# Keys and part of x transposed by DMA, and a rebuilt last batch, in a softcap attention with a routed attention layer behind it

## The chip, the cores and the metric

The kernel runs on one core of a Trainium2 chip. The metric is the device time of one execution in microseconds; a lower time is better. Engines are named as in the profile: PE is TensorE (the matrix engine) and PEld its weight loads, DVE is VectorE, ACT is ScalarE, POOL is GpSimd and SP is SyncE, whose queue issues nearly all DMAs.

## The reference

Two layers follow each other: softcap attention over 8 batches, 12 heads, 448 positions and 64 channels, and then a layer with four experts, each a small causal attention of its own, of which two are chosen for each token.

```python
scores = scale * np.matmul(q, k.transpose(0, 1, 3, 2))
scores = cap * np.tanh(scores / cap)
attn = softmax(scores)                       # max subtracted, sum + 1e-9
x = (attn @ v) laid out as [batch, 448, 12 * 64 = 768]

logits = x @ w_gate                          # 4 experts
topk = the two largest; w = softmax of these two
for e in range(4):
    q, k, v = x @ wq[e], x @ wk[e], x @ wv[e]
    a = softmax(causal(scale * q @ k.T))
    ye = a @ v @ wo[e]
    out += (e is chosen as first or second) * its w * ye
```

`out` is float32 of [8, 448, 768]. The inputs are float32; the kernel computes in float16 with float32 sums.

## The kernel before, in words

**Pairs.** The attention works on pairs of heads, six pairs to a batch, 48 in all. Pair p is step p of ACT, and two more steps follow (48 and 49, `NPV` is 50). For every step ACT runs three tanh (`tanh`, L768: the parts X, Y1 and Y2 of the scores) and one exp over all of them (`expo`, L780). The pairs of the last batch (42 to 47) only take 320 of their queries in their own steps (`W1`); the last 128 queries of all six are worked on in steps 48 and 49 (`pv2`).

**Feeding a pair.** `load` brings q, k and v of two pairs at once into a ring of four tiles each (`kf`, `qf`, `vf`); the last 64 keys come in small DMAs of their own (`ktf`, `vtf`). `cast` makes float16 of them on POOL. `tr` transposes the keys (`k16`, and `ktz` for the last 64) and the queries on PE into one PSUM bank; DVE copies the bank into `qk` in one instruction (L683). Rows were loaded so that one partition holds several neighbouring positions, and queries therefore stand permuted, within groups of 64, in `q16` and in `qk`. `fill` runs the score matmuls of a pair (`heads`, L717, and `tails`, L727).

**Finishing a pair.** `pv` multiplies the exps with the values (L795, L802) and DVE divides by the sum into `xk`. `xt` transposes `xk` on PE against a permutation that restores the order of the positions (`perm`, `pswap`, L841), and DVE copies the result into `xT` (L850), which holds one batch of x with channels on the partitions.

**The experts of a batch.** When a batch's six pairs are done, `b_v` (L910), `b_qk` (L937), `b_gate` and `b_mask` (POOL) prepare its values, keys, masked queries (`qm`, L951) and weights. The masks `mB` are transposed by a DMA into `mT` (`turned`, L389). Each batch has two expert score passes s = 0 and 1 (`b_score`, L1057), and each needs one ACT exp (L1066). The table `exps` says in which step of ACT these exps stand: for all but batch 6 five and six steps after the next batch begins, for batch 6 in steps 48 and 49. POOL zeroes what is not causal (`causal`, L1076, L1083). `b_pv` (L1116, L1131) gives `oB`, `b_ot` adds the two passes on POOL and has them transposed by DMA into `oT`, and `b_wo` (L1164) multiplies with wo: four tiles of 128 rows in two halves each, of which the last only stores its upper 64 rows because it overlaps the third. The results go through the four tiles `ob` to HBM (L1178).

**The last batch** has code of its own (`last`, `last2`, `normed`): projections (L1247, L1276, and L1390, L1400 for the last 128 rows), scores (L1300) on top of a mask that a matmul of `negm` puts into the bank first (L1290), exps (L1310), products (L1330, L1444), a division, transposes (L1208), a copy into `oTL` and the wo product (L1223). Its outputs go into the same tiles `ob` as batch 6's. Plain copies out of PSUM (`evac`, L377) go to DVE or, after ACT's fixed work, to ACT.

**The order.** Nothing is emitted in program order. Every operation goes into a graph (`Graph.op`) with an estimated cost. ACT's tanh and exp have a fixed order; all other operations get due times from it, partly given by hand as an offset to an ACT step (`due=(ref, ...)`). `solve` then simulates all engines and picks, for each, the ready operation that is due first. `SEEDS` and `JIT` add a pseudo-random offset to the due times, one seed for every 4 us of the simulated time. So a change of one cost or one operation moves the order of everything else. A DMA's simulated time is its wire time behind the DMAs before it (`wire`), and `occ` is its time on SP.

Of the kernel before, what the change touches and what calls it, by code (L numbers as in the profile page):

```python
# [16 lines left out]
SWITCH = 0.1  # L17
# [4 lines left out]
JIT = 0.784  # L22
SEEDS = (0, 0, 677, 325, 935, 794, 478, 0, 0, 908, 702, 455, 94, 0, 415, 476, 0, 612, 697, 64, 320, 0, 337, 707, 93, 0, 0, 917, 365, 771, 130, 0, 644, 11, 733, 810, 0, 8, 0, 0, 56, 391, 495, 0, 0, 0, 0, 0, 0, 579, 0, 0, 472, 59, 74, 554, 0, 0, 795, 949, 933, 285, 781, 323, 0, 548, 585, 976, 176, 0, 938, 86, 0, 0, 687, 0, 992, 980)
TWIRE = 0.2
TOCC = 0.18
# [3 lines left out]
KEEPN = 1  # L29
NFILL = 30  # L30
# [19 lines left out]
class Graph:  # L50
# [79 lines left out]
    def solve(self, when, banks, lent):  # L130
# [44 lines left out]
        while len(order) < n:  # L175
            best = None
            for e, rs in ready.items():
# [8 lines left out]
                def rank(x):  # L186
                    u = x[1]
                    if u.name[:4] == "gexp":
                        return -INF, 0.0, 0
                    d = u.due + lag if u.first or left < TAIL else max(u.due + lag, t0 + 1.223)  # L190
                    d -= 0.505 * (u.grp is not None and not u.opens and left >= TAIL)
# [5 lines left out]
                near = t0 + (0.007 if left >= TAIL else SWITCH + 0.02)  # L197
                t, o = min((x for x in c if x[0] <= near), key=rank)
                if e in ("PE", "DVE") and not o.first:
                    for t2, u in c:  # L200
                        if u.first and u.due + lag < t + o.occ + 0.0 and t2 < t + max(SWITCH + 0.01, min(o.occ, 0.25)):
# [68 lines left out]
def kernel(  # L270
# [116 lines left out]
    def turned(n, dst, src, r, w, name, due=None):  # L387
# [3 lines left out]
           wire=TWIRE * n, occ=0.4 + TOCC * n)  # L391
# [12 lines left out]
    vtz = [sb(f"vtz{i}", [128, 2, Dh + 1]) for i in range(NV)]  # L404
    qk = [sb(f"qk{i}", [128, S + 512]) for i in range(NQK)]
    yp = [sb(f"yp{i}", [128, 7, S]) for i in range(NYP)]
# [4 lines left out]
    xT = [sb(f"xT{i}", [128, NDC, S]) for i in range(2)]  # L411
# [7 lines left out]
    pB = [sb(f"pB{i}", [128, 64 + 1024]) for i in range(4)]  # L419
# [14 lines left out]
    negm = sb("negm", [128, W1])  # L434
# [6 lines left out]
    oTL = [sb(f"oTL{i}", [128, 2, 128]) for i in range(2)]  # L441
# [23 lines left out]
    def load(p, n):  # L465
# [13 lines left out]
        def tail(eng, dst, src, g):  # L479
# [4 lines left out]
        sp(lambda: full(kf[s][:, d], k[b, h, 0:KM], KC), w=w("kf"), name=f"ldk{p}", wire=0.8 * n)  # L484
        sp(lambda: nc_eng.dma_start(qf[s][:, d], q[b, h].rearrange("h (p c) d -> p h (c d)", c=QC)),
           w=w("qf"), name=f"ldq{p}", wire=0.95 * n)
# [8 lines left out]
        sp(lambda: full(vf[s][:, d], v[b, h, 0:KM], KC), w=w("vf"), name=f"ldv{p}", wire=0.8 * n)  # L495
# [39 lines left out]
    def setup_b():  # L535

# [21 lines left out]
        def lastc():  # L558
            nc.gpsimd.memset(vL[:, :, Dh : Dh + 1], 1.0)
            nc.gpsimd.memset(negm, 0.0)  # L560
# [3 lines left out]
        gp(0.9, lastc, w=["vL", "negm", "neg2"], due=150.0)  # L564
# [6 lines left out]
        gp(0.4, below(negm[:, 0:128], 0), ["negm"], ["negm"], due=150.0)  # L571
        gp(0.4, below(negm[:, W1 - 128 : W1], -64), ["negm"], ["negm"], due=150.0)
# [42 lines left out]
    def cast(p):  # L615
# [5 lines left out]

        def qc(e):
# [12 lines left out]
        gp(0.2, lambda: nc.gpsimd.tensor_copy(ktz[z], ktf[s][:, o].rearrange("p g d -> p (g d)")),  # L635
           [("ktf", x, 0), ("ktf", x, 1), ("zk", s)], [("ktz", z)], name=f"kt16_{p}")
# [10 lines left out]
    def tr(p):  # L647
# [29 lines left out]
        g = Group(AUX)  # L677
        pe(0, lambda: tk(g, (0, 1, 2)), kr + [("s", XB[0])] * (p == 1), [("tps", p, "k"), ("qkw", t)], g, occ=0.165, name=f"trk{p}")
# [27 lines left out]

    def heads(p, what):
        dst = X if what == "X" else Y
        ci = {"X": 0, "Y1": 1, "Y2": 2}[what]
        t = qk[of(p, what)[0] % NQK]  # L710
        n = wid(p)
        for c in (ci,) if p < NP else range(KC):
            for g in range(2):
# [4 lines left out]
                    dst[:, g, o], t[r, S + 128 * (c + 1) : S + 128 * (c + 2)], t[r, qs],  # L718
# [3 lines left out]
    def tails(p):  # L722
        for i, m in enumerate(of(p)):
# [3 lines left out]
            nc.tensor.matmul(X[:, 2, o], t[:, S : S + 128], t[:, qs], start=True, stop=True)  # L727

    def fill(p, what):
        def rd(p, what=None):  # L730
            return [y for m in of(p, what) for y in (
                ("qk", m % NQK, "k"), ("qk", m % NQK, "q"), ("qkw", m % NQK))]
# [12 lines left out]
        if what == "X":  # L745
            if p == 0:
                tr_first_tails()
            pe(wid(p), lambda: tails(p), rd(p) + [
                ("qk", m % NQK, "t") for m in of(p)], [("s", bs[2])], name=f"sT_{p}",
# [6 lines left out]
    exps = {HP * (b + 1) + (XOFF if b < LB - 1 else (6, 7))[s]: (b, s) for b in range(LB) for s in range(2)}  # L756
# [27 lines left out]
    def pv(p):  # L784
        if p >= NP:
            return pv2(p)
        y = yp[p % NYP]
# [3 lines left out]
        def mm(g, i, n, what):  # L791
            ps = bank(g)[:, 0 : 4 * (Dh + 1)].rearrange("p (n g d) -> p n g d", n=2, g=2)
            w = (WIN if p < PB else WIN1)[2 * i + n]
            if "X" in what:
                nc.tensor.matmul(  # L795
                    ps[:, n, :, :], y[:, 2, w : w + 128], vtz[u], start=(n == 0), stop=False,
# [3 lines left out]
            for c in cs:  # L800
                for h in range(2):
                    nc.tensor.matmul(  # L802
                        ps[:, n, h, :], y[:, SLOT[c][h], w : w + 128], v16[u][:, h, c, :],
# [3 lines left out]
        vr = [("v16", u), ("v16d", u), ("vtz", u), ("vtzd", u)]  # L807
# [23 lines left out]
    def xt(p, due=None):  # L831
        if p >= NP:
            return
        b, j = divmod(p, HP)
        g = Group(AUX)

        def mm():
            ps = bank16(g)
            for n in range(4 if p < PB else 3):
                w = 128 * n if p < PB else WIN1[n]  # L840
                nc.tensor.transpose(  # L841
                    ps[:, w : w + 128],
                    xk[p % NXK][:, n, :, :].rearrange("p g d -> p (g d)"),
                    perm if n < 3 else pswap,
# [8 lines left out]
    def pv2(p):  # L853
# [33 lines left out]
        def mt():  # L887
            for i in range(3):
                nc.tensor.transpose(
                    bank16(gt)[:, 128 * i : 128 * (i + 1)],  # L890
                    xk2[h][:, i].rearrange("p g d -> p (g d)"), perm)

        pe(0, mt, [("xk2", h), ("perm", 0), ("perm", 1)], [("xtp", p)], gt, occ=0.165, name=f"xt{p}")
# [8 lines left out]
    def b_v(b, ref):  # L902
        x = b % 2
        for n in range(4):
            g = Group(AUX + XB, 1.8)
            w = WIN[n]
            for j0 in (0, 2, 4):
                def mm(g=g, w=w, j0=j0):
# [8 lines left out]
                   due=(ref, 7.024 + 1.4 * n))  # L917
# [656 lines left out]
```

## Time and profile before

| what | value |
|---|---|
| median of 3 runs | 313.27 us (311.67 to 315.44) |
| the profiled execution | 314.04 us |
| its span | 312.0 us |
| busy share PE / DVE / ACT / POOL | 90% / 70% / 94% / 58% |
| mean granted clock of PE | 0.983 |
| read from HBM / written | 36.19 MB / 11.01 MB |

The span is the time from the first to the last thing that the profiler recorded; the profiled execution's own time has some 2 us around it. Busy shares are means over stages: the attention of 48 pairs fills the span but for a few microseconds ahead and the last batch's own work behind. In a row of the trace the first number is the start or a window, and a bracket at the end gives the idle time before the instruction and who ended it.

### The profile page before, as it was taken

Reading aid. Unit: us, or ns where it says so; the run is one execution under the profiler, and the core shown is the slowest. Engines: PE = TensorE matmul, PEld = TensorE weight load, DVE = VectorE, ACT = ScalarE, POOL = GpSimd, SP = SyncE. Lnnn points to the kernel's source line nnn. Section 1 sums busy time; section 2 is a strip of 40 time slices with the busy share of each in tenths; the row PEclk is TensorE's granted clock in tenths of the full one; section 3 lists DMA queues with packets and bytes.
Section 4 is the critical chain, followed back from the end, with each engine's and each line's share of the span. In section 5 each row is a group of like instructions: output and inputs, shape, how many; then the busy total and the mean of one; then the engine's idle time right before and its main releaser. Section 6 shows DMA issues by size and latency. Waiting matters only on the chain.

```text
span 312.0 us, 8950 instructions
## 1 busy us (share of the span) xinstructions
PE 280.9 (90%) x3476; PEld 190.4 (61%) x3476; DVE 217.8 (70%) x645; ACT 291.8 (94%) x246; POOL 181.4 (58%) x498
## 2 busy tenths in 40 slices
PE   7677689979898899989998999999999989999993
PEld 3354356658564766657655776568664866667761
DVE  2345556666764886869766877788776877786883
ACT  4699999998999999999999999999999999999562
POOL 7694436996787452984785576947866414701200
PEclk9979979998999999999999999999999999999999
DMA  6899999869976995789873698855014200531136
GB/s 183 182 227 221 297 272 253 220 168 268 251 189 159 313 272 159 187 179 255 217 164 78 201 310 196 129 162 154 2 41 146 97 2 19 87 120 60 36 148 207
DMA packets 87482, 53.29 MB, mean 171 GB/s; under 512 B 48144, under 2 KB 83728, under 8 KB 87440
## 3 DMA queue, kind: packets, MB, share of 16 engines
q1 hardware_dynamic: 87136, 52.49, 65.5%
q8 instruction: 27, 0.44, 0.6%
q10 hardware_dynamic: 304, 0.23, 0.2%
q14 instruction: 15, 0.12, 0.2%
HBM read 36.19 MB, written 11.01 MB: 151 GB/s over the span
## 4 chain that ended last, share of the span: by engine, by line
ACT 66%; PE 20%; DMA 4%; POOL 3%; issue 3%; DVE 2%; SPq 1%; ACTq 0%; POOLq 0%
ACT yp L768 34%; ACT yp L780 28%; ACT pB L1066 4%; PE A L1164 2%; DMA kf<-in_k_dram 2%; PE Y L717 2%; PE A L937 2%; PE A L910 2%; PE A L802 2%; DMA out_dram<-ob 2%; PE X L1057 1%; PE A L1116 1%; PE A L663 1%; PE A L795 1%; PE X L727 1%
## 5 line engine op out<-in xcount | busy, mean ns | idle before, releaser
L780 ACT ACTIVATE yp<-yp 128x3136 f16<-128x3136 f16 (+4 forms) x51 | 139.0, 2726 | 0.0
L768 ACT ACTIVATE yp<-Y 128x896 f16<-128x896 f32 (+2 forms) x100 | 94.6, 946 | 2.6 <-PE Y L717 2.6
L768 ACT ACTIVATE yp<-X 128x1344 f16<-128x1344 f32 (+2 forms) x50 | 65.1, 1302 | 2.5 <-PE X L727 1.5
L802 PE MATMUL A<-v,yp 128*128 128x65 f16 x1116 | 56.4, 194 | 0.0
L802 PEld LDWEIGHTS <-yp 128*128 128x128 f16 x1116 | 49.0, 98 | 5.7 <-issue 2.9
L795 PE MATMUL A<-vtz,yp 128*128 128x130 f16 x186 | 41.3, 222 | 7.9 <-ACT yp L780 3.7
L826 DVE TENSOR_TENSOR xk<-A,rca 128x256 f16<-128x256 f32 (+1 forms) x96 | 39.7, 415 | 2.9
L717 PE MATMUL Y<-qk 64*128 64x448 f16 (+2 forms) x216 | 36.2, 341 | 5.7 <-ACT yp L768 5.1
L639 POOL CAST v<-vf 128x384 f16<-128x384 f32 x48 | 24.6, 514 | 27.0 <-PE A L802 22.1
L620 POOL CAST k<-kf 128x384 f16<-128x384 f32 x47 | 23.7, 513 | 24.2 <-PE A L663 15.0
L683 DVE COPY qk<-A 128x960 f16<-128x960 f16 x47 | 29.5, 650 | 6.1 <-PE A L653 6.0
L377 DVE COPY ob<-A 128x384 f32<-128x384 f32 (+1 forms) x56 | 30.4, 554 | 4.7 <-PE A L1164 2.9
L823 DVE RECIPROCAL rca<-A 128x4 f32<-128x4 f32 (+1 forms) x96 | 17.1, 178 | 21.0 <-PE A L802 19.4
L795 PEld LDWEIGHTS <-yp 128*128 128x128 f16 x186 | 18.1, 97 | 19.7 <-ACT yp L780 9.3
L623 POOL CAST q<-qf 112x512 f16<-112x512 f32 x44 | 27.2, 619 | 2.3 <-DMA qf<-in_q_dram 2.1
L717 PEld LDWEIGHTS <-qk 64*128 64x128 f16 x324 | 15.0, 93 | 21.7 <-issue 15.5
L1164 PE MATMUL A<-wo,oT 128*128 128x384 f16 x112 | 26.2, 326 | 1.4 <-DVE xT L850 0.5
L1131 DVE SCALAR_TENSOR_TENSOR oB<-A,rcb,mw 128x256 f16<-128x256 f32 x54 | 25.5, 481 | 1.8
L850 DVE COPY xT<-A 128x448 f16<-128x448 f16 (+1 forms) x48 | 18.0, 376 | 9.9 <-PE A L841 9.5
L1141 POOL TENSOR_TENSOR oS<-oB,oB 128x512 f16<-128x512 f16 x14 | 16.1, 1154 | 14.5 <-DVE oB L1131 8.7
L1116 PE MATMUL A<-vB,pB 128*128 128x260 f16 x133 | 22.2, 275 | 1.6 <-DVE oB L1131 1.2
L653 PE MATMUL A<-ident,q 112*128 112x112 f16 x192 | 22.5, 219 | 0.0
(210 smaller groups left out, 569.8 us busy)
## 6 DMA issues: line engine op xcount, KB each, us to landing
qf<-in_q_dram SPq DMA_DIRECT2D x23, 448.0 KB, 6.0
kf<-in_k_dram SPq DMA_DIRECT2D x23, 384.0 KB, 5.2
vf<-in_v_dram SPq DMA_DIRECT2D x23, 384.0 KB, 4.9
out_dram<-ob SPq DMA_DIRECT2D x23, 384.0 KB, 3.8
out_dram<-ob SPq DMA_DIRECT2D x9, 192.0 KB, 2.9
ktf<-in_k_dram SPq DMA_DIRECT2D x46, 32.0 KB, 4.9
vtf<-in_v_dram SPq DMA_DIRECT2D x46, 32.0 KB, 4.3
ob<-in_moe_wv_dram SPq DMA_DIRECT2D x2, 384.0 KB, 4.1
```

Of the source, the lines that this page charges most:

```text
L377: (nc.scalar.copy if o.eng == "ACT" else nc.vector.tensor_copy)(dst(), src())
L623: e(q16[i], qf[s][:, h].rearrange("p h (c d) -> p c h d", c=QC))
L683: lambda: nc.vector.tensor_copy(qk[t], bank16(g)[:, 0 : S + 512]),
L717: nc.tensor.matmul(dst[:, g, o], t[r, S + 128 * (c + 1) : S + 128 * (c + 2)], t[r, qs], start=True, stop=True,)
L768: ACTS[what, p] = act(c_act(n * (b - a)), lambda: nc.scalar.activation(y[:, a:b, 0:n], src[:, 0 : b - a, 0:n], AF.Tanh, scale=isc / capf), ...
L780: act(c_act(n * (b - a), False), lambda a=a, b=b, n=n: nc.scalar.activation(y[:, a:b, 0:n], y[:, a:b, 0:n], AF.Exp, scale=capf), ks, ks, f ...
L795: nc.tensor.matmul(ps[:, n, :, :], y[:, 2, w : w + 128], vtz[u], start=(n == 0), stop=False, skip_group_check=True,)
L802: nc.tensor.matmul(ps[:, n, h, :], y[:, SLOT[c][h], w : w + 128], v16[u][:, h, c, :], start=False, stop=(c == 2), skip_group_check=True,)
L826: dve(c_dve(128 * m), lambda g=g, i=i, rc=rc, m=m: nc.vector.tensor_tensor(xk[p % NXK][:, 2 * i : 2 * i + m, :, :], view(g)[:, 0:m, :, 0:D ...
L1116: nc.tensor.matmul(bank(g)[:, 0 : E * (Dh + 1)], pB[pi][:, o : o + 128], vB[x][:, c, :, :], start=(t == 0), stop=(t == len(cs) - 1),)
L1131: dve(c_dve(E * Dh) + 0.06, lambda g=g, k_=k_, n=n: nc.vector.scalar_tensor_tensor(oB[s][:, n, :, :], view(g)[:, :, 0:Dh], rcb[k_][:, 0, : ...
L1164: nc.tensor.matmul(bank(g)[:, 0 : D // 2], oT[x][n // 2][:, r, n % 2, :], wo2[r][:, c0:c1], start=(r == 0), stop=(r == 1),)
```

## The change

- **Keys.** From pair 10 on (`KD`) the casts write both pairs' keys into one tile `kz`, and one DMA (`turned` with eight blocks of 128x128) transposes it into `kd`; PE then transposes only the queries, and DVE copies 448 columns in place of 960. 19 such DMAs. From pair 36 on (`NAT`) this copy writes with a stride and so puts the queries back into the order of their positions.
- **x.** From pair 36 on `pv` takes the rows in that order, in four tiles of 128 (the last reads 64 columns past the end, which `ypad` fills), so that `xk` needs no permutation any more. Ten pairs (36 to 46, not 41, not 47) are transposed by a DMA from SP, of four or three blocks; 41 and 47 stay on PE, with the identity.
- **Masks of the last batch.** The matmuls of `negm` (L1290) go; POOL zeroes what is not causal behind the exps, three selects for each of two groups of experts.
- **Outputs of the last batch** go into the tiles of `kf` in place of `ob`.
- **A shared product.** `b_wo` of batch 6 stops after three tiles. The 64 rows that are left are put into the unused half of the last batch's third `oTL` by a POOL copy; one product serves both.
- **Steps of expert exps.** Batch 5's move from the offsets 5 and 6 to 4 and 6, batch 6's from 6 and 7 to 5 and 6 (steps 47 and 48).
- **Order.** New `SEEDS`, `JIT`, wire times, due offsets and thresholds in `solve`.

```diff
-JIT = 0.784
+JIT = 0.549
-SEEDS = ...
+SEEDS = ...
-TWIRE = 0.2
-TOCC = 0.18
+TWIRE = 0.065
+NAT = 36
+KD = 10
...
-           wire=TWIRE * n, occ=0.4 + TOCC * n)
+           wire=TWIRE * n, occ=1.25)
...
+    kz = [sb(f"kz{i}", [128, 2, 512]) for i in range(2)]
+    kd = [sb(f"kd{i}", [128, 2, 512]) for i in range(3)]
...
+        def kcast(p):
+            s, o, x, j = p // 2 % NST, p % 2, p % (2 * NST), p // 2
+            dst = kz[j % 2][:, o]
+            gp(0.45, lambda: nc.gpsimd.tensor_copy(
+                dst[:, 128:].rearrange("p (c h d) -> p c h d", h=2, d=Dh),
+                kf[s][:, 2 * o : 2 * o + 2].rearrange("p h (c d) -> p c h d", c=KC)),
+                [("kf", x)], [("kz", j % 2, o, "k")], name=f"k16_{p}")
+            gp(0.2, lambda: nc.gpsimd.tensor_copy(
+                dst[:, 0:128], ktf[s][:, o].rearrange("p g d -> p (g d)")),
...
-        else:
+        elif p < KD:
             gp(0.45, lambda: kc(nc.gpsimd.tensor_copy), *kio, name=f"k16_{p}")
+        elif p % 2 == 0:
+            kcast(p)
+            kcast(p + 1)
+            j = p // 2
+            turned(8, lambda: kd[j % 3].rearrange("p o c -> p (o c)"),
+                   lambda: kz[j % 2].rearrange("p o c -> p (o c)"),
+                   [("kz", j % 2, o_, y) for o_ in range(2) for y in "kt"], [("kd", j % 3)],
+                   f"kT{p}")
...
+        if p >= KD:
+            pe(0, lambda: tq(g, 0, 2), [("q16", i), "ident"], [("tps", p, "q")], g, occ=0.1,
+               name=f"trq{p}")
+            pe(0, lambda: tq(g, 2, 4), [("q16", i), "ident"], [("tps", p, "r")], g, occ=0.1)
+            def qe():
+                dst, src = qk[t][:, 0:S], bank16(g)[:, 0:S]
+                if p >= NAT:
+                    dst = dst.rearrange("m (g t c) -> m g c t", c=QC, t=16)
+                    src = src.rearrange("m (g c t) -> m g c t", c=QC, t=16)
+                nc.vector.tensor_copy(dst, src)
...
-    exps = {HP * (b + 1) + (XOFF if b < LB - 1 else (6, 7))[s]: (b, s) for b in range(LB) for s in range(2)}
+    late = {5: (4, 6), 6: (5, 6)}
+    exps = {HP * (b + 1) + o: (b, s) for b in range(LB) for s, o in enumerate(late.get(b, XOFF))}
...
-            w = (WIN if p < PB else WIN1)[2 * i + n]
+            w = 256 * i + 128 * n if p >= NAT else WIN[2 * i + n]
...
+        if p >= NAT and p not in (PB - 1, NP - 1):
+            turned(nb, lambda: xT[b % 2][:, j, 0 : 128 * nb],
+                   lambda: xk[p % NXK][:, 0:nb].rearrange("p n g d -> p (n g d)"),
+                   [("xk", p % NXK, 0), ("xk", p % NXK, 1)], [("xT", b % 2, j)], f"xT{p}",
+                   due=due)
+            return
...
-                   due=(ref, 7.024 + 1.4 * n))
+                   due=(ref, 4.896 + 1.4 * n))
...
-        for n in range(4):
+        for n in range(4 if b < LB - 1 else 3):
...
+        o, u = kf[n].rearrange("p h x -> p (h x)"), n % 3
...
+        if n == 2:
+            y = (LB - 1) % 2
+            gp(0.25, lambda: nc.gpsimd.tensor_copy(oTL[u][:, :, 0:64], oT[y][1][:, :, 1, 64:128]),
+               [("oT", y, 1)], [("oTL", u, 1)], name="oT6")
...
-            for e in (1, 0):
-                n = 128 if part == 0 else W1
-                pe(n, lambda e=e, n=n: nc.tensor.matmul(
-                    bank(g2[e])[:, 0:n], ident, negm[:, 0:n], start=True, stop=False,
-                    skip_group_check=True), ["negm", "ident", ("kB", x, r)],
-                    [("sL", r, part, e)], g2[e], name="mk")
...
+            for o, base in ((64 + W1 * part, 0), (64 + W1 + 192, -64))[0 : 1 + part]:
+                def below(o=o, base=base):
+                    blk = pP[r][:, :, o : o + 128]
+                    nc.gpsimd.affine_select(
+                        out=blk, in_=blk, compare_op=ALU.is_ge, fill=0.0, base=base,
+                        pattern=[[0, 2], [1, 128]], channel_multiplier=-1)
+
+                gp(0.38, below, [], [("pB", pi, part) for pi in (2 * r, 2 * r + 1)], name="diagL")
...
-                xt(p - 1, (ACTS["Y1", p], 4.87))
+                xt(p - 1, (ACTS["Y1", p], 4.777))
...
-                        b_wo(bb, ACTS["Y1", p], *((12.261, 1.8) if bb < LB - 1 else (10.346, 0.5)))
+                        b_wo(bb, ACTS["Y1", p], *((13.885, 1.8) if bb < LB - 1 else (18.835, 0.5)))
```

More of the change, by code (lines that the diff above doesn't have):

```diff
@@ L189, in rank @@
                         return -INF, 0.0, 0
-                    d = u.due + lag if u.first or left < TAIL else max(u.due + lag, t0 + 1.223)
-                    d -= 0.505 * (u.grp is not None and not u.opens and left >= TAIL)
+                    d = u.due + lag if u.first or left < TAIL else max(u.due + lag, t0 + 1.145)
+                    d -= 0.233 * (u.grp is not None and not u.opens and left >= TAIL)
                     k = SEEDS[int(t0 / 4.0)] if t0 < 4.0 * len(SEEDS) else 0
@@ L200, in solve @@
                     for t2, u in c:
-                        if u.first and u.due + lag < t + o.occ + 0.0 and t2 < t + max(SWITCH + 0.01, min(o.occ, 0.25)):
+                        if u.first and u.due + lag < t + o.occ + 0.197 and t2 < t + max(SWITCH + 0.01, min(o.occ, 0.25)):
                             t, o = t2, u
@@ L440 @@
         "p (e c t) -> p e c t", e=E, c=4)
-    oTL = [sb(f"oTL{i}", [128, 2, 128]) for i in range(2)]
+    oTL = [sb(f"oTL{i}", [128, 2, 128]) for i in range(3)]
     gt1 = [sb(f"gt1_{i}", sh, f32) for i, sh in enumerate(
```

105 lines of the change are left out of this document (62 added, 43 removed).

## The prediction

> **What bounds the kernel now.** I read the page's busy line first, then the busy time by stage, then ScalarE's (ACT's) instructions in order of time, then the chain of work that ended last.
>
> ```profile
> span 312.0 us, 8950 instructions
> PE 280.9 (90%) x3476; PEld 190.4 (61%) x3476; DVE 217.8 (70%) x645; ACT 291.8 (94%) x246; POOL 181.4 (58%) x498
> ```
>
> By stage (columns: window, its length, busy us of PE, PEld, DVE, ACT and POOL with their counts, granted clock, DMA share, GB/s):
>
> ```profile
> 20.00:140.00 120.00, 106.90 (x1298) 71.42 (x1295) 79.80 (x230) 119.05 (x88) 79.66 (x213) 0.97 0.91 228
> 140.00:260.00 120.00, 114.16 (x1475) 79.75 (x1472) 94.71 (x272) 119.78 (x92) 74.22 (x182) 1.00 0.54 140
> 260.00:290.00 30.00, 28.71 (x396) 20.29 (x397) 22.14 (x74) 29.34 (x29) 9.95 (x27) 1.00 0.29 74
> 290.00:301.00 11.00, 11.00 (x123) 7.51 (x119) 8.92 (x36) 5.93 (x17) 2.26 (x2) 1.00 0.12 27
> 301.00:312.00 11.00, 6.17 (x73) 3.69 (x72) 6.02 (x19) 4.62 (x10) 0.00 (x0) 0.98 0.72 250
> ```
>
> From 20 to 290 us ACT is idle for 0.95 + 0.22 + 0.66 = 1.83 us of 270: it is the bound, and its tanh and exp are not touched. From 290 on it is half idle: first PE is busy without a gap (11.00 of 11.00), then nothing is.
>
> ACT in order of time, at the places that matter:
>
> ```profile
> 75.00 1.29 ACT L768 ACTIVATE yp<-X 128x1344 f16<-128x1344 f32 x1 [0.95 <-PE X L717]
> ...
> 249.71 1.11 ACT L768 ACTIVATE yp<-X 128x960 f16<-128x960 f32 x1
> ...
> 280.13 1.02 ACT L1066 ACTIVATE pB<-X 128x1024 f16<-128x1024 f32 x1 [0.66 <-PE X L1057]
> ...
> 289.16 0.88 ACT L780 ACTIVATE yp<-yp 128x768 f16<-128x768 f16 x1
> ```
>
> The row at 249.71 is the first narrow tanh, pair 42. That at 280.13 is the first of the two expert exps of batch 6 (the second follows one step later), and the last attention exp ends at 289.16 + 0.88 = 290.04. So 312.0 - 290.04 = 22 us are a tail that ACT does not bound. The end of the chain says what holds it last:
>
> ```profile
> 301.51 4.89 DMA out_dram<-ob
> ...
> 306.98 0.38 ACT oTL L377
> 307.37 0.04 issue
> 307.41 0.84 PE A L1223 x4
> ```
>
> A store of batch 6 takes 4.89 us, and batch 7's copy into the same `ob` tile waits for it.
>
> **The change, part by part.** The sum is made against the profiled execution's own 314.04 us (its span of 312.0 and 2.0 around it). That stands 0.77 above the median of 313.27.
>
> *Keys and x by DMA.* For 38 pairs PE loses four key transposes, for ten pairs three or four of x, and the evacuation shrinks.
>
> ```profile
> 277.25 0.17 PE A L841 x3
> ```
>
> ```profile
> L683 DVE COPY qk<-A 128x960 f16<-128x960 f16 x47 | 29.5, 650 | 6.1 <-PE A L653 6.0
> ...
> L674 DVE COPY qk<-A 128x448 f16<-128x448 f16 x1 | 0.4, 392 | 0.7 <-PE A L653 0.7
> ```
>
> A transpose is worth 0.17 / 3 = 0.057 us of PE: 38 x 4 x 0.057 = 8.7 us, and for x 35 x 0.057 = 2.0 us. DVE gains 26 x (0.650 - 0.392) = 6.7 us. The strided copy of the last twelve pairs isn't in the trace; between 0.392 and the wide 0.650 it loses nothing. But all this is taken off engines that stand beside a full ACT. It can buy at most the 1.83 us of ACT's stalls. I take 0.6, most of the 0.95 before the X heads at 75.00, and nothing of the rest.
>
> What it adds lies on SP's queue and the DMA engines: 19 transposes of eight blocks for keys and 10 of three or four for x. The trace has both sizes, `mT` (eight) and `oT` (four). Of `mT`, issue on SP and landing:
>
> ```profile
> L389 SPq DMA_TRANSPOSE mT<-mB x14: 1232/1258/2520, 60.1 to 269.4; - x14
> ...
> DMA to landing us min/median/max: 2.7/2.8/4.7
> ```
>
> And the DMA queue in two quiet stretches, the first from 222 to 232 us with two `oT`, the second from 255 to 275 with two of each (packets, MB, share of 16 engines):
>
> ```profile
> q1 hardware_dynamic: 1056, 0.26, 11.6%
> q1 hardware_dynamic: 3200, 0.79, 22.7%
> ```
>
> One `oT` is 0.116 x 10 / 2 = 0.58 us of all engines, one `mT` (0.227 x 20 - 1.16) / 2 = 1.69. The keys add 19 x 1.69 = 32 us of transfer over some 200 us, about 0.16 on the shares of 0.91 and 0.54. That is much up to 140 us, little after. On SP they cost 19 x 1.26 = 24 us of issue and those of x at most 10 x 1.26 = 13. A key turn now waits on SP for four casts of POOL; behind it stand the loads of later pairs, and for those wait POOL's casts. What covers this is the lead of the loads:
>
> ```profile
> 210.00 0.48 SPq L485 DMA_DIRECT2D qf<-in_q_dram  x1
> ```
>
> That is the last load, of pairs 46 and 47, at 210 us, while ACT is about (249.7 - 210) / 5.9 = 7 pairs before pair 42 (42 pairs in 249.7 us, 5.9 each). Eleven pairs of lead swallow a turn of 2.8 us. I cost it at nothing. If the cover is gone, each late turn costs ACT 4.7 - 2.8 = 1.9 us.
>
> The Trainium skill, "VectorE: DVE Perf Modes", The three transpose paths and Rules for kernel authors, speaks against this part: it gives 390 ns for a 128x128 block on TensorE and 1309 ns by DMA, and prefers TensorE where the result may land in PSUM. If blocks went one after another at that price, a key turn would take an estimated 8 x 1.31 = 10.5 us. The trace doesn't agree: eight blocks land in 2.8 us. It would make the slow rival below likelier, and I give it no more than the rows do.
>
> *Batch 6 one step earlier.* Its exps move from ACT's steps 48 and 49 to 47 and 48. ACT's own sum stays. What moves is PE work out of 283 to 290:
>
> ```profile
> 282.52 1.01 PE A L1116 x9
> ...
> 284.25 0.56 PE X0X1s L1057 x10
> ```
>
> 18 score matmuls at 0.056 and ten products at 0.112 are 2.1 us. In their place batch 7's projections can run, which now stand after 290 in the gapless stretch. Worth 0 (if DVE holds that stretch: 8.92 of 11) to 2.1; I take 1.5, as PE is nearest to full.
>
> *Masks on GpSimd.* PE loses eight mask matmuls; POOL gains six selects on 128x256.
>
> ```profile
> 290.00:301.00 11.00, 1.26 (x8) 0.61 (x8) 1.00 0.12 27
> ```
>
> ```profile
> L567 POOL TENSOR_SCALAR_AFFINE_SELECT negm<-negm 128x128 f16<-128x128 f16 x2 | 0.6, 294 | 0.1
> ```
>
> The first row is line 1290 alone: 1.26 us at most. A select is 0.29 to twice that, and POOL is idle there, but two stand between the last exps and the products: up to 1.2 us. Net -1.2 to +1.26 with either as bound; I take a gain of 0.5, since exps and products of that stage are apart by more than a select now.
>
> *One product shared.* Four of batch 6's sixteen wo matmuls and two copies go.
>
> ```profile
> 298.62 1.08 PE A L1164 x6
> ```
>
> 4 x 0.18 = 0.7 us of a full PE; a small POOL copy comes in its place. 0 to 0.7, I take 0.5.
>
> *Outputs in tiles of k.* What stands where the store's wait ends:
>
> ```profile
> 305.40 0.42 DVE L1201 TENSOR_TENSOR oB<-X2s,slL 128x256 f16<-128x256 f32 x1
> 305.58 0.48 ACT L377 COPY ob<-A 128x384 f32<-128x384 f32 x1 [1.09 <-DMA out_dram<-ob]
> ...
> 306.26 0.28 PE L1208 MATMUL A<-ident,oB 128*128 128x128 f16 x2
> ```
>
> The last tile's `oB` ends at 305.82, its transposes start at 306.26, its `oTL` at 306.98, behind the delayed `ob` copies. Without the wait the transposes start about 0.4 earlier and `oTL` right behind them, 306.54 or so less those 0.4: 0.84 us. With the 1.09 of the first copy it could be 1.9. I take 0.9. The larger worth is that without it the store would pin the end and the other gains would not show.
>
> The sum: 0.6 + 1.5 + 0.5 + 0.5 + 0.9 = 4.0 us, so 314.04 - 4.0 = 310.0, and 309.3 against the median. The bounds: gains together 1.83 + 2.1 + 1.26 + 0.7 + 1.9 = 7.8 (305.5 against the median), and at the other end 1.2 lost, 0.4 gained (314.1). The new seeds and jitter reorder everything else; the size of that I can't read, and I let it widen the range.
>
> **The rivals.** *Given back on ACT (24%).* Batch 6's first exp is now asked for about 5 us earlier, near 275.
>
> ```profile
> 274.72 1.16 DVE L951 TENSOR_TENSOR qm<-A,mT 128x448 f16<-128x448 f32 x2 [0.79 <-PE A L937]
> ```
>
> Its masked queries end only at 275.88, and 18 score matmuls at 0.056 take 1.0: ready at 276.9. If the lighter PE and the earlier due times don't bring this forward, ACT stands 2 us there, perhaps a little more for the scores queued behind. Then 4.0 - 2.0 to 3.0 leaves 1 to 2 us: 311.3 to 312.3, within 1%. For it speaks that ACT already waits 0.66 there today; against it that PE sheds seven transposes, 0.4 us, in each pair ahead of it.
>
> *Late keys, slower (14%).* Key turns queue behind loads on SP and on DMA engines near full (0.91 + 0.16 up to 140 us), and X heads wait on ACT's path. At 1.9 us each it cancels the gain from two late turns of 19 on and is slower by over 1% from four. With five late it is 309.3 + 9.5 = 318.8. The share speaks for it; the eleven pairs of lead against it. The page's rule above would lead here too.
>
> *More than forecast (12%).* Every term of the tail at its upper bound: 305.5. For it speaks that the tail has PE idle for 4.8 of the last 11 us; against it the chain of pair 49, which starts at 290 whatever is moved.
>
> *The forecast (50%)* is 309.3, its own range 306.5 to 312.
>
> **How the numbers follow.** One per cent, 3.1 us, is about what a measurement of this kernel can tell from no change: faster means below 310.1. Of the forecast's 50, 44 lie below and 6 within; of the ACT rival 22 within and 2 slower; of late keys 14 slower; of the upper bounds 12 faster. Together 0.56, 0.28 and 0.16. The range from 304.8 to 316 leaves out most of the late keys and a little beyond the upper bounds, under 2 in 10.
>
> **What would show it.** Right: from 20 to 290 ACT idle for no more than 2 us, key turns landing in about 3 us, no ACT wait on `kd`, the last attention exp ending at 289 to 290, a tail of 18 to 20 us, no wait on `out_dram<-ob` in it. Wrong: a wait of over 1 us before batch 6's first exp near 275 (given back), waits of X heads on DMA (late keys), the tail at 22 us with the products waiting on POOL's selects (no gain), or a tail under 17.

## The result and the profile after

The changed kernel is slower: a median of 328.43 us of 4 runs (327.19 to 332.81) against 312.47 us for the kernel before in the same session, a ratio of 1.048 [1.038, 1.059]. The forecast was 309.3, its range ended at 316. Ratios and their intervals, here and below, leave out runs that lie more than 1.5% above the fastest of the same kernel, while medians and ranges are of all its runs. The profiled execution of the changed kernel took 332.81 us, above its other three (327.2 to 329.4), so its rows are read for where the time went and the ratios for how much.

The busy line, and the same stages as before, with one more window for the longer tail (columns as before: window, length, busy us of PE, PEld, DVE, ACT, POOL, granted clock, DMA share, GB/s):

```profile
span 331.1 us, 8568 instructions
PE 280.3 (85%) x3277; PEld 180.2 (54%) x3277; DVE 212.6 (64%) x633; ACT 292.9 (88%) x246; POOL 182.9 (55%) x506
```

```profile
20.00:140.00 120.00, 97.61 (x1137) 62.00 (x1136) 69.01 (x214) 108.92 (x81) 72.93 (x197) 0.94 1.03 234
140.00:260.00 120.00, 107.61 (x1263) 69.81 (x1260) 86.44 (x241) 114.79 (x85) 75.46 (x192) 0.97 0.70 167
260.00:290.00 30.00, 25.41 (x282) 16.52 (x282) 21.16 (x61) 25.15 (x25) 9.66 (x23) 0.89 0.27 60
290.00:301.00 11.00, 10.49 (x156) 7.52 (x156) 8.68 (x25) 10.40 (x10) 3.19 (x10) 1.00 0.63 148
301.00:312.00 11.00, 10.66 (x161) 8.12 (x159) 9.31 (x38) 10.00 (x11) 3.32 (x5) 1.00 0.32 88
312.00:331.00 19.00, 12.73 (x147) 7.96 (x145) 10.42 (x38) 9.93 (x25) 2.34 (x6) 0.96 0.41 146
```

PE has 199 fewer matmuls and still as many busy microseconds as before, at a lower granted clock (0.94, 0.97 and 0.89 in the first three windows, against 0.97, 1.00 and 1.00). Its largest group of matmuls (the exps times the values) nevertheless took 195 ns each at the mean, against 194 before. ACT's busy total is nearly unchanged (292.9 against 291.8), but from 20 to 290 us it is idle for 11.08 + 5.21 + 4.85 = 21.1 us, where it was 1.83. That is as much as the whole loss (331.1 - 312.0 = 19.1). ACT in order of time, at the places that answer to those of before:

```profile
109.41 0.92 ACT L815 ACTIVATE yp<-Y 128x896 f16<-128x896 f32 x1 [2.20 <-PE Y L762]
...
296.50 1.02 ACT L1120 ACTIVATE pP<-X 128x1024 f16<-128x1024 f32 x1 [0.60 <-PE X L1111]
...
308.09 2.59 ACT L827 ACTIVATE yp<-yp 128x1920 f16<-128x1920 f16 x2
```

The last attention exp ends at 310.68, against 290.04: 20.6 us later. Behind it come 331.10 - 310.68 = 20.42 us of tail, against 21.96. So the attention lost 20.6 us and the tail gained 1.5. ACT's waits, first of the kernel before, then of the changed one (engine, line, whom it waited for: total us, times, longest):

```profile
ACT yp L768 <- PE Y L717: 2.6, 2, 1.7
```

```profile
ACT yp L815 <- PE Y L762: 16.3, 14, 3.1
ACT pP L1120 <- PE X L1111: 5.1, 4, 2.5
```

ACT waits for score matmuls. What those stood behind is in the list of all engines' waits and in the chain of work (start, length, what):

```profile
POOL kz L631 <- DMA kd<-kz: 19.1, 7, 5.3
DVE qm L1005 <- DMA mT<-mB: 6.8, 4, 2.8
PE A L1218 <- DVE qm L1005: 5.7, 3, 2.7
```

```profile
99.28 5.04 DMA mT<-mB
104.34 1.16 DVE qm L1005 x2
...
106.15 0.83 PE A L1218 x4
...
108.88 0.49 PE Y L762 x2
```

This is the pattern of the loss. The masks' transpose lands after 5.04 us; DVE stands at the masked queries `qm`, which need it; PE stands 2.7 us at a wo product (L1218), which the row puts down to `qm`, and both work on the PSUM tiles `A`; and two score matmuls of the attention, behind this product and others in PE's queue, end only at 109.37, when ACT had been idle for some 2.2 us. Each engine works through its queue in the order of the plan here, so one late transfer stops work that has nothing to do with it. Issue and landing of the eight-block transposes, keys and masks:

```profile
L390 SPq DMA_TRANSPOSE kd<-kz x19: 1231/1279/3555, 48.2 to 269.8; - x19
...
DMA to landing us min/median/max: 3.1/4.4/6.1
```

```profile
L390 SPq DMA_TRANSPOSE mT<-mB x14: 1237/1268/2360, 57.1 to 290.0; - x14
...
DMA to landing us min/median/max: 2.7/3.5/5.2
```

The masks took 2.8 us at the median before and now take 3.5; the keys take 4.4 where I had put 2.8.

### The profile page after: what moved, and what is told of

It reads as the page before. It is cut to its first block, busy times and chain, and to the rows that moved or that the text cites. A ratio compares the mean times of both kernels' runs of the same rounds, so it can differ in the third digit from the quotient of the medians.

```text
span 331.1 us, 8568 instructions
## 1 busy us (share of the span) xinstructions
PE 280.3 (85%) x3277; PEld 180.2 (54%) x3277; DVE 212.6 (64%) x633; ACT 292.9 (88%) x246; POOL 182.9 (55%) x506
## 4 chain that ended last, share of the span: by engine, by line
PE 39%; DMA 15%; ACT 12%; POOL 11%; DVE 9%; SPq 7%; issue 4%; POOLq 0%; DVEq 0%
ACT yp L815 7%; DMA qf<-in_q_dram 6%; PE A L1218 5%; PE A L850 5%; ACT yp L827 4%; DMA mT<-mB 4%; PE A L991 4%; PE Y L762 4%; PE A L964 4%; SPq L485 4%; DVE qk L715 3%; PE A L842 3%; PE X L1111 3%; DMA kf<-in_k_dram 2%; SPq L481 2%
## 5 line engine op out<-in xcount | busy, mean ns | idle before, releaser
L815 ACT ACTIVATE yp<-Y 128x896 f16<-128x896 f32 (+2 forms) x100 | 92.4, 924 | 16.3 <-PE Y L762 16.3
L1218 PE MATMUL A<-wo,oT 128*128 128x384 f16 x108 | 27.7, 365 | 7.9 <-DVE qm L1005 5.7
L378 DVE COPY ob<-A 128x384 f32<-128x384 f32 (+1 forms) x50 | 27.2, 555 | 9.0 <-PE A L1218 8.0
L762 PE MATMUL Y<-qk,kd 64*128 64x448 f16 (+2 forms) x176 | 29.6, 346 | 1.6 <-ACT yp L815 1.2
L631 POOL CAST kz<-kf 128x384 f16<-128x384 f32 x38 | 18.8, 506 | 21.1 <-DMA kd<-kz 19.1
L715 DVE COPY qk<-A 128x448 f16<-128x448 f16 x38 | 23.0, 627 | 8.9 <-PE A L681 4.8
L1170 PE MATMUL A<-vB,pP 128*128 128x260 f16 x137 | 23.6, 282 | 5.8 <-POOL pP L1130 4.1
L964 PE MATMUL A<-wvg,xT 128*128 128x260 f16 x168 | 24.2, 288 | 1.2 <-DVE qk L715 0.7
L681 PE MATMUL A<-ident,q 112*128 112x112 f16 x192 | 18.6, 213 | 5.3 <-POOL q L641 2.4
L1005 DVE TENSOR_TENSOR qm<-A,mT 128x448 f16<-128x448 f32 x28 | 16.3, 618 | 10.2 <-DMA mT<-mB 6.8
L1195 POOL TENSOR_TENSOR oS<-oB,oB 128x512 f16<-128x512 f16 x14 | 16.1, 1154 | 10.5 <-issue 7.7
```

What stands on the lines that cost most here:

```text
L378: (nc.scalar.copy if o.eng == "ACT" else nc.vector.tensor_copy)(dst(), src())
L715: nc.vector.tensor_copy(dst, src)
L762: nc.tensor.matmul(dst[:, g, o], kT[r, 128 * (c + 1) : 128 * (c + 2)], t[r, qs], start=True, stop=True,)
L815: ACTS[what, p] = act(c_act(n * (b - a)), lambda: nc.scalar.activation(y[:, a:b, 0:n], src[:, 0 : b - a, 0:n], AF.Tanh, scale=isc / capf), ...
L964: nc.tensor.matmul(bank(g)[:, 0 : E * Dh + E], xT[x][:, j, w : w + 128], wvg[:, j, :], start=(j == 0), stop=(j == NDC - 1),)
L1218: nc.tensor.matmul(bank(g)[:, 0 : D // 2], oT[x][n // 2][:, r, n % 2, :], wo2[r][:, c0:c1], start=(r == 0), stop=(r == 1),)
```

## The experiments

Two theories came first. *Crowding*: the added transposes delay the transfers beside them. *Order*: the new settings of the planner (seeds, thresholds, due offsets, and the figures by which it counts a DMA) give a worse order, whatever the parts of the change do. A third, *tiles*, was that two `kz` and three `kd` are too few, since POOL waits 19.1 us for a `kz` to come free. All ratios are against the kernel before, with 95% intervals. Each run has a short name, e or s with a number, given with its result; in the s runs the order of before is kept.

**Parts of the change taken back, in its own order.** Keys back on PE:

```diff
-KD = 10
+KD = 48
```

> All keys transposed by PE again; x from pair 36 on by DMA, the last batch, the steps of the expert exps and the new order's settings stay. Crowding (19 key transposes on SP's queue and on full DMA engines, landing in 4.4 us where mT alone took 2.8, hold up GpSimd, PE and then ScalarE): ScalarE's stalls from 20 to 290 us fall from some 20 us to under 4, time 308 to 313, and the shorter tail shows as a small gain. Order (the new seeds, due times and expert steps fit badly whatever transposes the keys): stays above 322. Plan and tiles: back to 308 to 315 too, since no key DMA is left.

e1: 329.91 us, 1.049 [1.041, 1.057]: nothing comes back. (From pair 36 on the bank is copied in two instructions here, since x still goes by DMA.) The landings of `mT` and `oT` are those of before again (medians 2.8 and 2.4 us), yet PE waits for `oT` and ACT for PE:

```profile
ACT yp L824 <- PE Y L771: 13.4, 10, 4.3
...
PEld L1227 <- DMA oT<-oS: 7.6, 4, 3.8
...
PE A L1227 <- DMA oT<-oS: 5.8, 3, 3.6
```

So the keys' transposes as the sole cause fall. Keys by DMA only from pair 36 on:

```diff
-KD = 10
+KD = 36
```

> Keys by DMA only from pair 36 on, 6 transposes in place of 19, when nearly all loads are done. Crowding: about as without any, 309 to 315, since the DMA engines are at 0.3 then. Tiles (two kz and three kd tiles make SP and GpSimd wait in their order, loads or not): a part of the loss stays, 314 to 319, with waits of kz casts on kd in the late part. Order: above 322.

e2: 336.18 us, 1.075 [1.069, 1.081]: with a third of the transposes it is slower still. A time that moves by 2.7% the wrong way shows how much a new order alone can do. More tiles:

```diff
-    kz = [... for i in range(2)]
-    kd = [... for i in range(3)]
+    kz = [... for i in range(4)]
+    kd = [... for i in range(5)]
```

> As changed, with four kz tiles in place of two and five kd tiles in place of three. Tiles: GpSimd's 19 us of waiting for kd<-kz and SP's 13 us of waiting for the score matmuls go, time 312 to 320. Crowding: the same bytes go through the same engines, 322 to 330. Order: any, 320 to 335.

e4: 333.53 us, 1.068 [1.062, 1.073]: no gain, though POOL's wait for a `kz` falls from 19.1 to 4.4 us. So the tile theory falls: POOL's 19 us are not what ACT pays for. And the planner's time for a transpose set back:

```diff
-TWIRE = 0.065
+TWIRE = 0.2
```

> As changed, but the plan counts 0.2 us of wire per block again in place of 0.065, so an eight-block transpose lands in 4.15 us by the plan instead of 3.07 (measured: 4.4). Plan (the order is built on transposes that are 1.3 us too fast, so everything behind them is asked for too early): 312 to 320. Crowding: the transfers are still there, 322 to 330. Order: any, 320 to 335.

e3: 323.68 us, 1.036 [1.031, 1.042]: 4.7 us of the medians come back by one figure that changes no instruction, only their order. The intervals overlap, and e2 shows a new order move the time by more, so the waits are the better sign. They fall where the late transfers stood:

```profile
ACT yp L815 <- PE Y L762: 8.9, 9, 2.8
...
DVE qm L1005 <- DMA mT<-mB: 0.5, 1, 0.5
```

DVE's wait for the masks was 6.8 us, ACT's for the Y scores 16.3.

**Order and parts apart.** The kernel before with nothing but the change's settings of the order:

```diff
-JIT = 0.784, SEEDS, TWIRE = 0.2, occ=0.4 + 0.18 * n
+JIT = 0.549, new SEEDS, TWIRE = 0.065, occ=1.25
...
 (and the change's thresholds, load wire times and due offsets)
```

> The kernel before with nothing changed but the settings of the order: seeds, jitter, thresholds, due offsets, wire times and SP's time per transpose of the change. Order (what costs the time is an order that the engines, taking their instructions in turn, can't keep; the parts of the change matter little): 320 to 335 without a single key transposed by DMA. Crowding (key transposes on SP and the DMA engines): 310 to 316.

e5: 327.04 us, 1.047 [1.041, 1.052]: a loss of the same size, without one part of the change. Its stalls are not all in the same places, though:

```profile
ACT yp L767 <- PE A L801: 6.2, 2, 3.2
...
DVE qm L950 <- DMA mT<-mB: 0.7, 1, 0.7
```

DVE hardly waits for masks, and two of ACT's stalls, 6.2 us together near 280 and 287 us, end with a product of values (L801). The reverse, the changed kernel with the settings of before (only the due offset of batch 6's wo product kept at 18.835):

> The changed kernel with the settings of the order of before, as far as they exist there. Order: old settings don't fit the new graph either, since the seeds work on operation numbers: 320 to 335. If it was the new settings as such that are bad: 308 to 316. Crowding: 320 to 335 as well.

e6: 323.77 us, 1.036 [1.032, 1.040]. So settings made for the one kernel don't suit the other, and this pair alone does not tell what the parts are worth. Two ways lead on: keep the order of before operation by operation, or take the seeds out of both kernels.

**The order of before, kept.** In these kernels the planner still sees the operations of before; where one isn't needed, nothing is emitted in its place. First the outputs of the last batch in `kf`, then the masks by POOL's selects as well:

```diff
-        o = ob[n]
+        o = kf[n].rearrange("p h x -> p (h x)")
```

> The kernel before, its order kept operation by operation; only the last batch's outputs go into the tiles of kf in place of ob. The prediction's term is 0.9 us (0.4 to 1.9): about 312.0 where before has 313, no ScalarE wait on out_dram<-ob left. If the wait was covered: no difference.

> As the one before, and the eight mask matmuls of the last batch are left out for six selects on GpSimd behind the exps, order kept. The prediction's terms together are 1.4 us: about 311.6. If the selects stand in the way of the products: up to 1.2 us slower than with the tiles alone.

s2: 313.15 us, 1.000 [0.997, 1.003], and s3: 312.56 us, 0.999 [0.996, 1.002]. The first one's ACT copies at the end:

```profile
304.30 0.48 ACT L377 COPY kf<-A 128x384 f32<-128x384 f32 x1 [0.88 <-DVE slL L1199]
305.06 0.47 ACT L377 COPY kf<-A 64x384 f32<-64x384 f32 x1 [0.29 <-PE A L1223]
305.56 0.37 ACT L377 COPY oTL<-A 128x256 f16<-128x256 f16 x1
```

The wait on the store is gone and the last `oTL` starts at 305.56, where it started at 306.98. This trace is 0.9 us shorter than that of before (311.1 against 312.0), but the profiled execution of before stood 0.77 above its median; over all runs the two kernels take the same time.

Keys from pair 10 on by DMA, PE's key transposes left out, tiles enough (4 and 5):

> The kernel before, its order kept operation by operation; only the keys from pair 10 on go by DMA: the casts write kz (four tiles), each fourth cast is followed by a transpose of eight blocks on SP into kd (five tiles), PE's key transposes are empty and the copy is 448 wide. Order: keys by DMA cost little by themselves, 309 to 317. Crowding: 322 to 335, with ScalarE waiting for X and Y heads that wait for kd.

s1: 323.43 us, 1.032 [1.028, 1.036]. The chain of work names who is late; the profiled execution took 331.50 us, over 6 us more than the next of its five runs, so its durations are on the long side:

```profile
136.56 5.74 DMA mT<-mB
...
167.49 7.16 DMA oT<-oS
...
207.36 7.31 DMA oT<-oS
214.72 1.46 PE A L1197 x4
```

Not the keys, which nothing in the chain waits for, but the experts' own transposes, two of them over 7 us. They have no lead. The same for the keys of the last twelve pairs only, six transposes, of which the first is issued at 186 us:

```diff
-KD = 10
+KD = 36
```

> The kernel before, order kept, keys by DMA only from pair 36 on (six transposes, when nearly all loads are done). Crowding by the loads: 311 to 315, about as before. If transposes of keys cost about 0.5 us each wherever they stand: 316.

s5: 313.36 us, 1.000 [0.998, 1.002]: no harm, and no gain that can be told from the work taken off PE and DVE. Next the transposes as pure load: all of PE's work is done as before, and 19 eight-block transposes whose results nobody reads are added on SP where the keys' would stand:

> The kernel before, order kept, keys transposed by PE as before; beside them SP issues the 19 eight-block transposes of the change from zeroed tiles into tiles that nobody reads. Crowding of SP and the DMA engines as such: 319 to 326, with the wo products and the masked queries of the experts waiting for oT and mT that land in 4 us and more, as with the keys by DMA in the kept order (323). If it is the wait for the keys themselves: 312 to 315.

s4: 325.21 us, 1.037 [1.034, 1.041]. And the same with one block each, so that SP issues as many but the engines move an eighth:

> As the kernel with unread transposes (325), but each of the 19 turns one block of 128x128 in place of eight. If the bytes on the DMA engines do the harm: 312.5 to 316, a small part of the loss. If SP's issue, over 1.2 us whatever the size, and the order of its queue do it: 320 to 326.

s6: 1.002 [0.997, 1.008]. This ratio rests on the lower four of ten runs; the ten spread from 311.80 to 319.14 us with a median of 317.79, and all of them together would give 1.010. So most of the 3.7% comes with the transfers and not with SP's issue; whether the issue costs nothing or up to 1% is open. In the kernel with the eight-block ones (waits and `oT`'s landing):

```profile
POOL q L646 <- DMA qf<-in_q_dram: 9.2, 5, 3.4
...
PEld L1187 <- DMA oT<-oS: 6.2, 4, 2.3
```

```profile
DMA to landing us min/median/max: 2.3/3.8/6.4
```

POOL waited 2.1 us for `qf` in the kernel before; `oT` landed in 2.4. Crowding is real where the order does not reckon with it, but e5 loses as much without one added transpose.

**No seeds.** With `JIT = 0` the planner follows its own due times. First what the seeds are worth to the kernel before: without any, and with those of the change.

```diff
-JIT = 0.784
+JIT = 0.0
```

> The kernel before with jitter zero, so the seeds do nothing. Order: the seeds of before are worth much, 316 to 332. If the plan is good without them: 311 to 315.

> The kernel before with the seeds and the jitter of the change, its thresholds and due offsets kept. If the seeds are what makes an order good or bad: 316 to 328, with the new order alone at 327. If the thresholds and due offsets did the harm there: 312 to 316.

e8: 318.61 us, 1.021 [1.016, 1.025], and e10: 319.2 us, 1.017 [1.013, 1.022]. So its own seeds are worth about 2% to it, and foreign ones no more than none. Now the changed kernel without seeds, first with its own settings, then with those of before:

> The changed kernel with jitter zero: its seeds do nothing, its thresholds, due offsets and wire times stay. If its seeds are what fits badly: 317 to 322, as with the old settings and no jitter (1.012 of before). If the wire time and thresholds do it: 324 to 330.

> The changed kernel planned with the settings of before and no jitter, to stand beside the kernel before without jitter (318.6). If the change itself is at fault when no seeds favour either: 324 to 332. If only the seeds and settings are: 314 to 320.

e7: 332.91 us, 1.063 [1.056, 1.069], and e9: 320.18 us, 1.012 [1.003, 1.021], a ratio that rests on two of its four runs (315.60 and 319.54 us; all four would give 1.019). Two more kernels split these. In the second, only the planner's figures for a transpose are changed to those of the change:

```diff
-TWIRE = 0.2
-TOCC = 0.18
+TWIRE = 0.065
...
-           wire=TWIRE * n, occ=0.4 + TOCC * n)
+           wire=TWIRE * n, occ=1.25)
```

> The changed kernel with the old settings and no jitter, only the plan's wire time per block 0.065 in place of 0.2 and SP's time per transpose 1.25. With wire 0.2 the change in its own order came down from 328 to 324. If a plan that counts transposes as too fast is harmful whatever the seeds: 321 to 326. If not: 316 to 320.

e12: 331.23 us, 1.058 [1.050, 1.067]: 4.65% of the time before, some 14.6 us, by how the planner counts a transpose (11.0 us by the medians). What is left to e7, the thresholds, due offsets and load wire times, is within the intervals. Waits with the long count (e9), then with the short one (e12):

```profile
POOL kz L632 <- DMA kd<-kz: 8.8, 5, 3.8
...
ACT yp L816 <- PE Y L763: 6.6, 5, 3.0
...
DVE qm L1006 <- DMA mT<-mB: 0.7, 1, 0.7
```

```profile
POOL kz L631 <- DMA kd<-kz: 12.3, 8, 4.7
...
DVE qm L1005 <- DMA mT<-mB: 10.0, 7, 2.1
ACT yp L815 <- PE Y L762: 9.8, 7, 2.8
```

DVE's wait for the masks goes from 0.7 to 10.0 us, and ACT's for PE follows. The transposes land at about the same times in both (keys 3.5 and 3.9 us at the median, masks 3.5 and 3.2): they did not become slower, their readers were put earlier. In the traces DVE comes to a batch's first masked queries 5.3 us after the issue of its first mask transpose with the long count and 3.0 us after it with the short one (medians of the seven batches).

The other kernels sort the same way. Seven were planned with the short count on the wire (the changed kernel, e1, e2, e4, e5, e7, e12): they stand at 1.047 to 1.075. Six were planned anew with the long one (e3, e6, e8, e9, e10, e11): they stand at 1.012 to 1.036. DVE's wait for `mT` and that of PE's weight loads for `oT` are together 10.0 to 12.3 us in the first seven, except for 3.5 in e5, and 0.2 to 1.9 us in the six. The last run takes the transposes of keys and x back to PE in the order with the long count:

```diff
-NAT = 36
-KD = 10
+NAT = 48
+KD = 48
```

> As the one before, without the transposes by DMA (keys and x on PE; x with the permutation again); the last batch, its output tiles, the shared product and the steps of the expert exps stay as changed. Crowding: 8 to 12 us below the kernel with them. The prediction's gain of 3.4 us in the tail would make it 315; if moving the steps costs what the tail gains: 318 to 320, as before without jitter.

e11: 318.54 us, 1.016 [1.011, 1.021], against 1.012 with them on the DMAs: where the plan counts a transpose long enough, moving them costs nothing that can be told, and gains nothing either.

## Why the prediction was wrong

**The account.** Along the chain of runs: the order of before without its seeds is +2.1% (e8); the parts of the change on top -0.9% (e9; its interval overlaps that of e8, so this isn't separated from nothing); the short count of a transpose +4.65% (e12); the rest of the change's settings, seeds among them, -1.0% (the changed kernel itself; intervals overlap). Together 4.8%, as the steps must, since each starts where the last one ended; another path through the runs would split it otherwise.

**The step that failed: "The new seeds and jitter reorder everything else; the size of that I can't read, and I let it widen the range."** It was the largest term by far: e5 makes it 14.6 us by its ratio, where all my terms together were 4.0. I let it widen the range and gave it no direction. And the part that decides could be read. I worked out from two quiet stretches that an eight-block transpose takes 1.69 us of all DMA engines. The planner before counted 8 x 0.2 = 1.6 for the same thing; the change sets 8 x 0.065 = 0.52. That line stood in the diff, beside my own number, and I didn't put one against the other. The landing of a single transpose would not have given it away: the plan's own sum for eight blocks is 2.2 + 0.52 + 0.35 = 3.07 us with the short count and 4.15 with the long one, and masks landed in 2.8 us before. It is behind other transfers that the short count is too early: in the changed kernel masks took 3.5 us and keys 4.4. A plan that counts a third of the transfer believes its queue empty when it is full, puts the readers of `mT` and `oT` too early, and the engines stop there, as the waits of the short-count kernels show. I read the diff for operations and passed over its constants as if they could only shuffle.

**"I cost it at nothing" (keys and x by DMA).** The working looked at the lead of the keys alone. It was right for them: in s1 the chain doesn't wait for keys. It left out who shares the engines without any lead. The masks' and outputs' transposes go out when they are ready and are waited for soon; in s1 and s4 these came late, in s4 the loads of q too, at a price of 10 and 12 us. I had put the share of the DMA engines at 0.91 + 0.16 up to 140 us and at 0.54 + 0.16 behind it, "little after"; in s4 it is 1.01 and 0.76 (to 260 us), and ACT is idle 5.7 us in the first stretch and 6.2 in the second. I added up the share and looked for the harm in the wrong transfer. The gain of 0.6 is not told from nothing either: the part of it that was run alone, s5, is 1.000 [0.998, 1.002].

One reading of this part was wrong outright: the strided copy of the last twelve pairs "loses nothing". In the changed kernel the row of these copies is

```profile
L715 DVE COPY qk<-A 128x448 f16<-128x448 f16 x38 | 23.0, 627 | 8.9 <-PE A L681 4.8
```

and its mean hides two kinds: 26 plain ones of 0.38 us at the median, and 12 strided ones of 1.13 to 1.18 us, nearly twice the wide copy's 0.65. The planner counts 0.54 for them. Those twelve lose most of what the 26 gain; e9 with them and e11 without them are not told apart.

**The rival "late keys"** had the right side and the right resource, but the wrong place and price: no X head stood waiting for `kd` in the waits of the changed kernel, and 318.8 us is 9.6 short of what came. The rule of the Trainium skill that I had set beside it ("VectorE: DVE Perf Modes", Rules for kernel authors, TensorE where PSUM may take the result) gives the right advice for the kept order from pair 10 on (s1, 1.032); from pair 36 on it makes no difference (s5, 1.000). My estimate from its 1309 ns a block, 10.5 us for eight in a row, is not borne out: eight land in 2.7 us at the least (`mT`).

**The rival "given back on ACT"** did not show: ACT waits 0.60 us before batch 6's first exp (the row at 296.50).

**The small terms.** *Outputs in tiles of k*, 0.9 us: s2 measures 1.000 [0.997, 1.003], 0.85 at most by its interval. The mechanism was as described, the wait left and `oTL` came 1.42 earlier in the trace; the end did not follow in the medians. *Masks on GpSimd*, 0.5: s3 against s2 is 0.6 us with overlapping intervals, not told from nothing. *Batch 6 one step earlier* and *the shared product* were not run alone; the tail as a whole became 1.5 us shorter, where the masks, the shared product, the output tiles and batch 6's step were to give 3.4. At its end stands now what is left of batch 6 itself (the chain of the changed kernel):

```profile
323.36 1.47 PE A L1218 x8
324.86 0.48 ACT ob L378
```

The last eight matmuls of its wo product, given a due offset of 18.835, are done after the last batch's products at L1284. The wait that the prediction named is gone, and another operation holds the end.

**Right**: that ACT bounds the kernel and that only its stalls count. Of the signs of being wrong that I listed none names what came, "waits of X heads on DMA" being the nearest; the first sign of being right, ACT idle for no more than 2 us from 20 to 290, is the one that caught it, with 21.1.

**Open.** The time on the wire and the time on SP (`occ`) were changed together in e12; e3 alone, where only the wire changes, gives 4.7 us back. That the readers placed too early are the way from the count to the stalls rests on the waits and on when DVE comes to its masks, not on a run that moves only the readers. e5 loses as much with few such waits, and e3 and e6 stay at 1.036 with hardly any (0.9 and 0.8 us): what those orders lose elsewhere was not traced. In e1 the landings are as short at the median as before and PE waits for `oT` nonetheless, up to 3.8 us; the longest landing there is 5.8 us, where the plan's own sum for four blocks (2.2 + 4 x 0.065 + 0.35) is 2.8; which of its instructions stand too early was not traced. Why the short count costs 4.65% but taking back the wire alone only 1.2% in the seeded order is not settled; those seeds go with the short count's order. No version beat the kernel before: s3, at 0.999, is not told from it.

## What to carry to other kernels

In a kernel whose order is planned ahead, read the diff's cost constants as you read its instructions: put each against what the trace shows for the thing that it stands for, for a transfer its share of the engines under load and not only its landing on a free queue, and ask which in-order engine will stand there if it is too short. When load is added to a shared queue, look first at the transfers on it that have no lead, not at the new ones. And compare two designs at a kept order or without seeds for either, because an order that suits one of them is worth 2% to it here, more than all the parts were to gain.

## What was not expected of the hardware

The DMA queue's page line, before and after (packets, MB, share of 16 engines):

```profile
q1 hardware_dynamic: 87136, 52.49, 65.5%
```

```profile
q1 hardware_dynamic: 112000, 58.62, 74.1%
```

The added transposes are 6.13 MB in 24864 packets. The changed kernel's DMA engines are busy for 0.741 x 331.1 - 0.655 x 312.0 = 41 us more, 6.7 us per MB added; the mix of before took 204 us for 52.49 MB, 3.9 us per MB. So a byte transposed occupied the engines some 1.7 times as long as a byte of that mix, if the other transfers took what they took before. The quiet stretch of the prediction (255 to 275 us), where transposes stand almost alone, gives 0.227 x 20 / 0.79 = 5.7 us per MB. The Trainium skill, "Advanced Engine Details and Errata", X-Bar Transpose (TRN2), has them "as fast as regular DMAs"; by either count the trace doesn't agree.

Nineteen such transfers that nobody reads cost 12 us of 313 (s4), while the same number of one-block ones cost 0.2% to 1% (s6). A four-block transpose that lands in 2.4 us at the median in the kernel before (5.7 at most) takes 3.8 in s4 (6.4 at most). A copy of 448 columns out of PSUM takes DVE 0.38 us when it writes them in a row and 1.15 us when it writes with a stride (medians of the changed kernel). And PE's granted clock was 0.89 in a stretch of the changed kernel (260 to 290 us) where the kernel before had 1.00 for the same window. How long PE was busy does not explain that alone: in the same window it was busy 26.6 us in e5, at 1.00, and 26.9 us in e12, at 0.83.
